# A retention-and-FFN kernel: scores of two rows in the FFN's PSUM banks, a new order in the attention bursts, and earlier loads of v

## The chip, the cores and the metric

The kernel runs on one core of a Trainium2 chip. The metric is the time of one execution on the device in microseconds (us); the figure of the kernel before is the median of three runs.

## The reference, cut to what matters

Inputs are q, k and v of shape (4 batches, 8 heads, 768 positions, 64) and two weight matrices, `w_in` (512 x 2048) and `w_out` (2048 x 512), all drawn in float32.

```python
for t in range(S):
    state = gamma * state + outer(k[t], v[t])       # per batch and head, 64 x 64
    y[t] = scale * q[t] @ state
x = y with the heads side by side                   # 3072 tokens x 512
h = x @ w_in
g = h * clip(h + 3.0, 0.0, 6.0) / 6.0
out = g @ w_out
```

## The kernel before, in words

**The work.** The 3072 tokens are cut into 24 rows of 128 (`NROW`), six rows to a batch (`ROWS_B`), and the rows into six units of four (`UR`, `NU`). The recurrence is done in chunks of 64 positions, two in a row: scores of k against q, a mask, products of masked scores with v (the inner part), products of q with the state from before (the outer part), and sums k x v that are added to the state. The FFN's first product is made for 16 blocks of 128 of the 2048 features and for six units of 512 tokens: 96 groups, each of 12 matmuls of 128x512 (`mm1`, L380: four blocks of the contraction times three products of a high and a low part). The second product (`mm2`, L479) is a blocked scheme with seven products per two units.

**The row's step.** `burst(r)` (L298) does the new part of row r and the old part of row r - 1 on TensorE. Its order before is: the outer part of the old row (`outer_part`, L232), a small matmul called `pace`, the scores of the new row (`scores`, L245), another `pace`, the inner part of the old row (`inner_part`, L257), then on VectorE `xr`, the old row's result times its decay (L321), split into a high part (ScalarE, L127) and a low part (VectorE, L128) of `x`; then the sums of the new row (`gather`, L269), the mask product `am` (VectorE, L335) and two additions to the state (`add_up`, L282: VectorE, L290; for the first row of a batch one copy on ScalarE, L292). Scores and sums of a row lie in one tile `sc` of two PSUM banks, from a pool with a single buffer.

**The FFN's first product.** `mm1` takes one tile `h` of one PSUM bank from the pool `ps_h`, which has three buffers (L90, L381). After its 12 matmuls ScalarE makes relu(h + 3) (L389), VectorE multiplies min(6 ., ...) by h (L390), and the result `g` is stored to DRAM. The next group's tile is another of the three buffers.

**Where the order comes from.** TensorE's order is written by hand: all of `advance` and `mm1` is issued in program order (L395). The first five bursts (rows 0 to 4) come before any group. The first four groups have a burst behind each of them. In units 0 and 1, whose 32 groups are interleaved, the bursts of rows 8 to 12 follow, in units 2 to 4 four bursts to a unit of 16 groups, and in unit 5 there are none. The other engines' orders are set when the program is built, by a scheduler that goes by the dependencies between tiles. All loads and stores are issued by SyncE.

**Early loads.** The first eight rows (`AHEAD`) are loaded at the start (`load`, L182): kt, qt, vn, kn of a row, 256 KB each, then the decay table `dq` of the row (`load_decay`, L213), and after rows 0, 2, 3 and 5 (`WITH`) one block of `w_in` of 512 KB (`fetch`, L96). For these rows ScalarE scales vn by a decay, eight instructions to a row (`decay`, L201). The blocks of `w_in` are turned into float32 and split (`build_w1`, L143: six instructions of VectorE and two of ScalarE); four of them are built between the first bursts, the others beside the groups.

Of the kernel before, what the change touches and what calls it, by code (L numbers as in the profile page):

```python
# [9 lines left out]
F32 = mybir.dt.float32  # L10
# [6 lines left out]
PSUM = bass.MemoryType.PSUM  # L17
DRAM = bass.MemoryType.DRAM

P = 128  # L20
# [8 lines left out]
def retention_ffn(ctx: ExitStack, tc: tile.TileContext, qkv, w_in, w_out, dvs, dqs, out, B, H, S, D):  # L29
# [6 lines left out]
    nc = tc.nc  # L36
# [6 lines left out]
    ROWS_B = S // P  # L43
    UR = 4
    UT = UR * P
    NU = NROW // UR
    WARM = 14
    AHEAD = 2 * UR
    WITH = (0, 2, 3, 5)
    BUFS = {"lkt": 1, "lqt": 2, "lvn": 2, "lkn": 1}  # L50
    SPARE = ("lkn", "lkt", "lqt", "lqt")
    BLK = 2 * P
# [11 lines left out]
    HALF = P // 2  # L64
# [11 lines left out]
    def nm(s):  # L76
        return f"{s}_{next(serial)}"
# [8 lines left out]
    ph1 = ctx.enter_context(ExitStack())  # L86
    wst = ph1.enter_context(tc.tile_pool(name="wst", bufs=1))
    xpool = ph1.enter_context(tc.tile_pool(name="xpool", bufs=2))
    hpool = ph1.enter_context(tc.tile_pool(name="hpool", bufs=3))
    ps_h = ph1.enter_context(tc.tile_pool(name="ps_h", bufs=3, space=PSUM))  # L90
    att = ctx.enter_context(ExitStack())
    apool = att.enter_context(tc.tile_pool(name="apool", bufs=2, side="right"))
    ps_a = att.enter_context(tc.tile_pool(name="ps_a", bufs=1, space=PSUM, side="right"))


    def fetch(src):  # L96
        st = wst.tile([P, src.shape[-1]], I64, tag="st", name=nm("st"), bufs=2)
        nc.sync.dma_start(out=st, in_=src)
        return st
# [69 lines left out]

    warm = apool.tile([P, 2, P], F32, tag="state", name="warm")  # L170
    nc.vector.memset(warm, 0.0)
    idle = ps_h.tile([P, UT], F32, tag="h", name="idle")
    for n in range(WARM):
        nc.tensor.matmul(idle[:, 0:P], warm[:, 0], warm[:, 1], start=True, stop=True)


    halves = [slice(h * D, (h + 1) * D) for h in range(2)]
# [4 lines left out]
    def load(r):  # L182

        t = rows[r] = {}
        if r < AHEAD and r % 2 == 0:
            early[r] = wpool.tile([P, 7, NPAIR, P], F32, tag="w", name=nm("early"), bufs=NSLOT - 1)
        for i, (x, n) in enumerate((("kt", 1), ("qt", 0), ("vn", 3), ("kn", 2))):  # L190
            o = r % 2 * 4 + i
            if r < AHEAD and o < 7:
                t[x] = early[r // 2 * 2][:, o]
            else:
                tag = SPARE[r // 2] if r < AHEAD else f"l{x}"
                t[x] = apool.tile([P, NPAIR, P], F32, tag=tag, name=nm(x), bufs=BUFS[tag])
            nc.sync.dma_start(out=t[x].rearrange("p h n -> p (h n)"), in_=qkv[r, n])
        if r >= AHEAD:
            decay(r)

    def decay(r):  # L201
        v = rows[r]["vn"].rearrange("p a (h e) -> p (a h) e", h=2)
        if r < AHEAD:
            for h in range(H):
                nc.scalar.activation(
                    out=v[:, h], in_=v[:, h], func=AF.Copy, scale=cst_sb[:, r % ROWS_B, h : h + 1]
                )
        else:
            nc.gpsimd.tensor_tensor(  # L209
                out=v, in0=v, in1=cst_sb[:, r % ROWS_B, :, None].to_broadcast([P, H, D]), op=ALU.mult  # L210
            )

    def load_decay(r):  # L213
        if r < AHEAD:
            if "dq" not in early:
                early["dq"] = wpool.tile([P, ROWS_B, NPAIR, P], F32, tag="w", name=nm("early"), bufs=NSLOT - 1)
            t = early["dq"][:, r % ROWS_B]
        else:
            t = apool.tile([P, NPAIR, P], F32, tag="dq", name=nm("dq"), bufs=1)
        rows[r]["dq"] = t  # L220
        if r < ROWS_B or r >= AHEAD:
            nc.sync.dma_start(out=t.rearrange("p h n -> p (h n)"), in_=dqs[r % ROWS_B])
# [22 lines left out]
    def scores(t):  # L245

        for i, c, a, h in tiles:
            nc.tensor.matmul(  # L248
                t["sc"][halves[h ^ a], a, i, c],
                t["kt"][halves[h], 2 * i + a, cut[c]],  # L250
                t["qt"][halves[h], 2 * i + a, cut[c]],
                start=True,
                stop=True,
                skip_group_check=True,
            )
# [13 lines left out]
    def gather(t, n):  # L269

        for i, c, a, h in tiles:
            if not c or n < ROWS_B - 1:
                nc.tensor.matmul(  # L273
                    t["u"][halves[h], a, c, i],
                    t["kn"][halves[h ^ a], 2 * i + a, cut[c]],
                    t["vn"][halves[h ^ a], 2 * i + a, cut[c]],
                    start=True,
                    stop=True,
                    skip_group_check=True,
                )  # L280
# [17 lines left out]
    def burst(r, new=True, old=True):  # L298

        new, old = new and rows.get(r), old and rows.get(r - 1)  # L300
        if old:
            ys = ps_a.tile([P, 2, UT], F32, tag="y", name=nm("y"))[:, :, 0 : 2 * P]
            old["y"] = ys.rearrange("p h (i n) -> p h i n", i=2)
            outer_part(old, (r - 1) % ROWS_B)
            pace()
        if new:
            sc = ps_a.tile([P, 2, 2, 4, HALF], F32, tag="sc", name=nm("sc"))
            new["sc"] = sc[:, :, 0].rearrange("p a (i c) n -> p a i c n", i=2)
            new["u"] = sc[:, :, 1].rearrange("p a (c i) n -> p a c i n", c=2)
            scores(new)  # L310
        if old:
            pace()
            inner_part(old)
            u, n = divmod(r - 1, UR)
            if u not in xs and u == 2:
                xs[u] = [wpool.tile([P, NK, UT], F32R, tag="w", name=nm("x"), bufs=NSLOT - 1) for a in range(2)]
            elif u not in xs:
                x = xpool.tile([P, 2, NK, UT], F32R, tag="x", name=nm("x"))
                xs[u] = [x[:, a] for a in range(2)]
            x = apool.tile([P, NPAIR, P], F32, tag="xr", name=nm("xr"))  # L320
            nc.vector.tensor_tensor(  # L321
                out=x.rearrange("p (h i) n -> p h (i n)", h=2),
                in0=ys,
                in1=old["dq"].rearrange("p (h i) n -> p h (i n)", h=2),
                op=ALU.mult,
            )
            hi, lo = (xs[u][a][:, :, n * P : (n + 1) * P] for a in range(2))
            split(hi, lo, x)
            del rows[r - 1]
        if new:  # L330
            gather(new, r % ROWS_B)
            if r in before:
                new["state"] = before.pop(r)
            new["am"] = apool.tile([P, 2, 2, 2, HALF], F32, tag="am", name=nm("am"), bufs=1)
            nc.vector.tensor_tensor(  # L335
                out=new["am"].rearrange("p a i c n -> p a (i c) n"),
                in0=sc[:, :, 0],
                in1=mask[:, None, None].to_broadcast([P, 2, 4, HALF]),
                op=ALU.mult,
            )  # L340
            add_up(r)

    def attention():

        st = []
        for r in range(AHEAD):
            load(r)
            load_decay(r)
            if r in WITH:
                st.append(fetch(w_in[len(st)]))  # L350
        decay(0)
        for r in range(NROW + 1):
            if r == AHEAD:
                burst(r, new=False)
                yield
                burst(r, old=False)
            else:
                burst(r)
            if st and r in (0, 2, 3, 4):
                build_w1(len(WITH) - len(st), st.pop(0))  # L360
            if r + 1 < AHEAD:
                decay(r + 1)
            if r >= AHEAD - 1 and r + 1 < NROW:
                load(r + 1)
            if AHEAD <= r < NROW:
                load_decay(r)
            yield

    gen = attention()
    done = 0  # L370

# [6 lines left out]


    def mm1(u, jj):  # L380
        h = ps_h.tile([P, UT], F32, tag="h", name=nm("h"))  # L381
        for k in range(NK):
            t, o = w1_block(jj, k)
            for n, (a, b) in enumerate(((0, 0), (0, 1), (1, 0))):
                nc.tensor.matmul(  # L385
                    h, t[:, o, a], xs[u][b][:, k], start=k + n == 0, stop=(k, n) == (NK - 1, 2), skip_group_check=True
                )
        g = hpool.tile([P, UT], F32, tag="g", name=nm("g"))
        nc.scalar.activation(out=g, in_=h, func=AF.Relu, bias=three)  # L389
        ins = nc.vector.scalar_tensor_tensor(out=g, in0=g, scalar=6.0, in1=h, op0=ALU.min, op1=ALU.mult)  # L390
        nc.sync.dma_start(out=gd[jj // 2][:, u, jj % 2], in_=g)
        return ins.ins
# [8 lines left out]
    advance(UR + 1)  # L401
    n_w1, n_w2 = len(WITH), 0
    for n, (u, jj) in enumerate(steps):
# [150 lines left out]
    for n, step in enumerate(work):  # L554
        b, s, j = step
# [95 lines left out]
```

## Time and profile before

| | |
|---|---|
| median of three runs (lowest, highest) | 593.75 us (593.53, 596.97) |
| the profiled execution | 594.2 us, of which the span of its instructions 592.4 us |
| TensorE matmul busy | 568.0 us, 96% of the span |
| VectorE busy | 438.1 us, 74% |
| ScalarE busy | 247.3 us, 42% |
| `mm1` matmuls (L385) | 1152, 271.1 us busy, from 32.2 to 355.2 us |
| `mm2` matmuls (L490) | 1008, 232.3 us busy, behind them |

The page's busy time of TensorE is modelled at its ends: a stream of matmuls overlaps, so 394 ns is the duration of one, not the step from one to the next. The idle time before an instruction is put down to what released it. Windows of the trace give the busy time of each engine in a stretch, with the clock that TensorE was granted (1.00 is full speed).

### The profile page before, as it was taken

The page shows a single profiled execution, that of the slowest core. Times are in us where ns is not written, and L with a number is a line of the kernel's source. Part 1 is how long each engine was busy: PE and PEld are TensorE (multiplying, and loading weights), DVE is VectorE, ACT ScalarE, POOL GpSimd, SP SyncE. Part 2 cuts the span into 40 slices and gives each one's busy share as a digit, 9 for nine tenths or more (in the row PEclk, how much of TensorE's full clock was granted, in tenths as well). Part 3 has the DMA queues.
Part 4 walks back from the last instruction along what each step waited for, and adds up shares of the span by engine and source line. Part 5 has one row for each costly group of instructions (what it writes and reads, how often), then busy time and mean ns, then how long its engine had stood idle before and what let it go on. Part 6 is the DMA issues. An engine that isn't in the chain of part 4 may idle for free.

```text
span 592.4 us, 13046 instructions
## 1 busy us (share of the span) xinstructions
PE 568.0 (96%) x5228; PEld 466.6 (79%) x5228; DVE 438.1 (74%) x790; ACT 247.3 (42%) x446; POOL 17.1 (3%) x22
## 2 busy tenths in 40 slices
PE   6787999898999999999999999999999999999997
PEld 5665788687888888888888886888888888888885
DVE  4869999999634499344436975999689966799853
ACT  5664445444322344222234544454444443444430
POOL 0001000000001000000000000000000000000000
PEclk8788999999999999999999999999999999999999
DMA  9966586665855557655445428984689635897002
GB/s 329 391 232 206 186 268 221 242 225 195 274 187 192 176 196 233 231 167 188 165 139 181 161 105 294 361 266 128 202 285 339 186 107 175 267 299 255 18 1 106
DMA packets 63564, 124.12 MB, mean 210 GB/s; under 512 B 7312, under 2 KB 7568, under 8 KB 63504
## 3 DMA queue, kind: packets, MB, share of 16 engines
q1 hardware_dynamic: 63216, 123.24, 61.9%
q8 instruction: 41, 0.67, 0.5%
q14 instruction: 19, 0.16, 0.1%
q10 hardware_dynamic: 288, 0.06, 0.0%
HBM read 91.81 MB, written 31.46 MB: 208 GB/s over the span
## 4 chain that ended last, share of the span: by engine, by line
PE 76%; DVE 16%; DMA 3%; issue 3%; ACT 1%; SPq 0%; DVEq 0%; ACTq 0%
PE o L490 38%; PE h L385 33%; DVE g L390 2%; DVE w L128 2%; DVE wb L115 2%; DVE we L118 2%; DVE ww L121 2%; PE y L236 1%; PE y L260 1%; PE sc L273 1%; PE sc L248 1%; DMA st<-in_w_in 1%; DVE we L109 1%; DVE wb L110 1%; DVE ws L80 1%
## 5 line engine op out<-in xcount | busy, mean ns | idle before, releaser
L385 PE MATMUL h<-x,w 128*128 128x512 f32 x1152 | 271.1, 394 | 4.7 <-DVE g L390 3.2
L385 PEld LDWEIGHTS h<-x,w 128*128 128x128 f32 x1152 | 215.2, 189 | 52.5 <-DVE g L390 4.7
L490 PE MATMUL o<-gc,w 128*128 128x512 f32 x1008 | 232.3, 392 | 1.4 <-ACT gc L127 1.0
L490 PEld LDWEIGHTS o<-gc,w 128*128 128x128 f32 x1008 | 189.1, 188 | 44.5 <-ACT gc L127 1.8
L390 DVE SCALAR_TENSOR_TENSOR g<-g,h 128x512 f32<-128x512 f32 x96 | 65.7, 685 | 80.7 <-ACT g L389 80.7
L389 ACT ACTIVATE g<-h,three 128x512 f32<-128x512 f32 x96 | 65.2, 684 | 97.4 <-PE h L385 91.6
L128 DVE TENSOR_TENSOR gc<-gr,gc 128x512 fp32r<-128x512 f32 x120 | 80.1, 691 | 22.1 <-ACT gc L127 21.8
L127 ACT ACTIVATE gc<-gr 128x512 fp32r<-128x512 f32 x120 | 71.9, 623 | 58.1 <-PE o L490 39.8
L127 ACT ACTIVATE gc<-keep 128x512 fp32r<-128x512 f32 x48 | 30.3, 633 | 62.8 <-PE o L490 45.0
L128 DVE TENSOR_TENSOR gc<-keep,gc 128x512 fp32r<-128x512 f32 x48 | 33.3, 695 | 13.5 <-ACT gc L127 13.4
L127 ACT ACTIVATE w<-ww 128x384 fp32r<-128x384 f32 (+2 forms) x34 | 18.8, 555 | 42.6 <-DVE ww L121 34.8
L113 ACT ACTIVATE we<-we,ebias 128x512 int32<-128x512 int32 x32 | 23.0, 718 | 20.2 <-DVE we L109 20.2
L127 ACT ACTIVATE x<-xr 128x512 fp32r<-128x512 f32 x24 | 15.1, 630 | 29.3 <-DVE xr L321 29.3
L507 DVE SCALAR_TENSOR_TENSOR u<-o,u 128x512 f32<-128x512 f32 (+1 forms) x31 | 20.1, 667 | 6.3 <-PE o L490 6.3
L209 POOL TENSOR_TENSOR vn<-vn,cst_sb 128x512 f32<-128x512 f32 x16 | 16.8, 1049 | 268.3 <-DMA vn<-in_qkv 268.3
L121 DVE SCALAR_TENSOR_TENSOR ww<-wb,we 128x512 f32<-128x512 f32 x32 | 22.8, 713 | 0.6
L115 DVE SCALAR_TENSOR_TENSOR wb<-st,wb 128x512 f32<-128x512 uint32 x32 | 22.9, 714 | 0.3
L335 DVE TENSOR_TENSOR am<-sc,mask 128x512 f32<-128x512 f32 x24 | 16.4, 684 | 8.5 <-PE sc L273 8.5
L128 DVE TENSOR_TENSOR w<-ww,w 128x384 fp32r<-128x384 f32 (+2 forms) x34 | 20.1, 594 | 3.3 <-ACT w L127 3.2
L118 DVE SCALAR_TENSOR_TENSOR we<-st,we 128x512 int32<-128x512 int32 x32 | 22.0, 687 | 0.1
L83 DVE TENSOR_TENSOR keep<-gr,gr 128x512 f32<-128x512 f32 x24 | 16.5, 694 | 5.7 <-DMA gr<-gd 5.7
L128 DVE TENSOR_TENSOR x<-xr,x 128x512 fp32r<-128x512 f32 x24 | 16.5, 688 | 2.7 <-ACT x L127 1.9
(48 smaller groups left out, 360.5 us busy)
## 6 DMA issues: line engine op xcount, KB each, us to landing
gr<-gd SPq DMA_DIRECT2D x168, 256.0 KB, 4.1
gd<-g SPq DMA_DIRECT2D x96, 256.0 KB, 2.7
st<-in_w_in SPq DMA_DIRECT2D x16, 512.0 KB, 4.3
st<-in_w_out SPq DMA_DIRECT2D x16, 512.0 KB, 4.4
early<-in_qkv SPq DMA_DIRECT2D x28, 256.0 KB, 6.0
kn<-in_qkv SPq DMA_DIRECT2D x20, 256.0 KB, 4.7
kt<-in_qkv SPq DMA_DIRECT2D x16, 256.0 KB, 4.3
qt<-in_qkv SPq DMA_DIRECT2D x16, 256.0 KB, 3.6
```

The lines of the kernel that those rows point to most:

```text
L113: nc.scalar.activation(out=e, in_=e, func=AF.Relu, scale=8.0, bias=ebias)
L115: nc.vector.scalar_tensor_tensor(out=y, in0=lo.bitcast(U32), scalar=2.0**-32, in1=b, op0=ALU.mult, op1=ALU.add)
L118: nc.vector.scalar_tensor_tensor(out=e, in0=hi, scalar=-2147483648, in1=e, op0=ALU.bitwise_and, op1=ALU.bitwise_or)
L121: nc.vector.scalar_tensor_tensor(out=w, in0=y, scalar=2.0**-20, in1=e.bitcast(F32), op0=ALU.mult, op1=ALU.mult)
L127: nc.scalar.activation(out=hi, in_=src, func=AF.Copy)
L128: nc.vector.tensor_tensor(out=lo, in0=src, in1=hi, op=ALU.subtract)
L209: nc.gpsimd.tensor_tensor(out=v, in0=v, in1=cst_sb[:, r % ROWS_B, :, None].to_broadcast([P, H, D]), op=ALU.mult)
L385: nc.tensor.matmul(h, t[:, o, a], xs[u][b][:, k], start=k + n == 0, stop=(k, n) == (NK - 1, 2), skip_group_check=True)
L389: nc.scalar.activation(out=g, in_=h, func=AF.Relu, bias=three)
L390: ins = nc.vector.scalar_tensor_tensor(out=g, in0=g, scalar=6.0, in1=h, op0=ALU.min, op1=ALU.mult)
L490: nc.tensor.matmul(banks[b, i, h], w2c[jj][:, RIGHT[i], a, h], gc[:, q, c], start=jj == 0 and n == 0, stop=jj == NFP - 1 and n == 2, skip_ ...
L507: nc.vector.scalar_tensor_tensor(out=out_[:, cut], in0=banks[b, i, h][:, cut], scalar=f, in1=other[:, cut], op0=ALU.mult, op1=ALU.add)
```

## The change

- Three one-bank tiles `h` become one tile `hs` of three banks, `[P, 3, 512]`, from the same pool with one buffer. `mm1` takes the slice `hs[:, n % 3]`, in turn. The warm-up matmuls write the third slice.
- Scores and sums of rows 1 and 3 lie in the first two slices of `hs`; all other rows keep the tile `sc`.
- A burst issues scores of the new row, outer part of the old row, `pace`, sums of the new row, `pace`, inner part of the old row.
- For rows 1 to 7 vn is loaded ahead of kt, qt and kn; `dq` of a row is loaded behind the next row's data; the blocks of `w_in` are fetched behind rows 1, 3, 4 and 6.

```diff
-    WITH = (0, 2, 3, 5)
+    WITH = (1, 3, 4, 6)
...
-    ps_h = ph1.enter_context(tc.tile_pool(name="ps_h", bufs=3, space=PSUM))
+    ps_h = ph1.enter_context(tc.tile_pool(name="ps_h", bufs=1, space=PSUM))
...
-    idle = ps_h.tile([P, UT], F32, tag="h", name="idle")
+    NH = 3
+    hs = ps_h.tile([P, NH, UT], F32, name="hs")
+    turns = iter(range(1 << 30))
     for n in range(WARM):
-        nc.tensor.matmul(idle[:, 0:P], warm[:, 0], warm[:, 1], start=True, stop=True)
+        nc.tensor.matmul(hs[:, NH - 1, 0:P], warm[:, 0], warm[:, 1], start=True, stop=True)
...
-        for i, (x, n) in enumerate((("kt", 1), ("qt", 0), ("vn", 3), ("kn", 2))):
-            o = r % 2 * 4 + i
+        parts = [("kt", 1), ("qt", 0), ("vn", 3), ("kn", 2)]
+        for i in (2, 0, 1, 3) if 0 < r < AHEAD else range(4):
+            (x, n), o = parts[i], r % 2 * 4 + i
...
         new, old = new and rows.get(r), old and rows.get(r - 1)
+        if new:
+            if r < UR and r % 2:
+                sc = hs[:, 0:2].rearrange("p a (b x n) -> p a b x n", b=2, n=HALF)
+            else:
+                sc = ps_a.tile([P, 2, 2, 4, HALF], F32, tag="sc", name=nm("sc"))
+            new["sc"] = sc[:, :, 0].rearrange("p a (i c) n -> p a i c n", i=2)
+            new["u"] = sc[:, :, 1].rearrange("p a (c i) n -> p a c i n", c=2)
+            scores(new)
         if old:
             ys = ps_a.tile([P, 2, UT], F32, tag="y", name=nm("y"))[:, :, 0 : 2 * P]
             old["y"] = ys.rearrange("p h (i n) -> p h i n", i=2)
             outer_part(old, (r - 1) % ROWS_B)
             pace()
         if new:
-            sc = ps_a.tile([P, 2, 2, 4, HALF], F32, tag="sc", name=nm("sc"))
-            new["sc"] = sc[:, :, 0].rearrange("p a (i c) n -> p a i c n", i=2)
-            new["u"] = sc[:, :, 1].rearrange("p a (c i) n -> p a c i n", c=2)
-            scores(new)
+            gather(new, r % ROWS_B)
         if old:
             pace()
             inner_part(old)
...
         if new:
-            gather(new, r % ROWS_B)
             if r in before:
                 new["state"] = before.pop(r)
...
             load(r)
-            load_decay(r)
+            if r:
+                load_decay(r - 1)
             if r in WITH:
                 st.append(fetch(w_in[len(st)]))
+        load_decay(AHEAD - 1)
         decay(0)
...
     def mm1(u, jj):
-        h = ps_h.tile([P, UT], F32, tag="h", name=nm("h"))
+        h = hs[:, next(turns) % NH]
```

How the change moves instructions is seen in the built programs' orders. In them a name is a tile with its number, `x16` counts equal rows that follow each other, and the brackets name the engines' counters for which a row waits (`DVE_49` is VectorE's, `Activation_49` ScalarE's, `PE_49` TensorE's own, `DMAHW` a transfer's).

The first place is TensorE from the end of the first group on, through the burst of row 5, to the second group. Before:

```order
L236 MATMUL y_638<-early_149,state_498 64x64 [waits PE_49]
L236 MATMUL y_638<-early_149,state_498 64x64 x3
L236 MATMUL y_638<-early_149,state_595 64x64 [waits DVE_49]
...
L230 MATMUL pace_655<-mask 64x4
L248 MATMUL sc_657<-early_149 64x64 [waits DMAHW6_49,DMAHW7_49,DVE_49,PE_49]
L248 MATMUL sc_657<-early_149 64x64 x15
L230 MATMUL pace_674<-mask 64x4 [waits PE_49]
L260 MATMUL y_638<-am_593,early_149 64x64 x16
L273 MATMUL sc_657<-early_149,kn_158 64x64 [waits DMAHW1_49,DMAHW0_49]
L273 MATMUL sc_657<-early_149,kn_158 64x64 x7
L385 MATMUL h_730<-x_286,w_20_229 128x512 x12
```

Now:

```order
L251 MATMUL sc_635<-early_146 64x64 [waits DMAHW6_49,DMAHW7_49,DVE_49,PE_49]
L251 MATMUL sc_635<-early_146 64x64 x15
L239 MATMUL y_652<-early_146,state_496 64x64 [waits PE_49]
...
L233 MATMUL pace_669<-mask 64x4
L276 MATMUL sc_635<-early_146,kn_157 64x64 [waits DMAHW5_49,DMAHW0_49]
L276 MATMUL sc_635<-early_146,kn_157 64x64 x7
L233 MATMUL pace_679<-mask 64x4 [waits PE_49]
L263 MATMUL y_652<-am_591,early_146 64x64 x16
L394 MATMUL hs<-x_301,w_20_229 128x512 [waits DVE_49]
L394 MATMUL hs<-x_301,w_20_229 128x512 x11
```

Scores moved to the front and sums ahead of the inner part; the second group, which waited for nothing of its own, now waits for VectorE. The count of VectorE's work that this wait names is reached with `g_631`, the `g` of the first group. So it is for every later group: in the built program the wait of each of the groups 2 to 96 names the count at which the `g` of the group just before it is finished. Before, a group's wait, where it has one, names the `g` of three groups earlier.

The second place is VectorE in the early rows, where `we`, `wb` and `ww` are the steps of building a block of `w_in`. Before, from the state of row 1 to that of row 2:

```order
L290 TENSOR_TENSOR state_309<-sc_251,state_218 128x256
L290 TENSOR_TENSOR state_311<-sc_251,state_309 128x256
L109 TENSOR_SCALAR we_402<-st_139 128x512
L110 TENSOR_SCALAR wb_401<-st_139 128x512
L115 SCALAR_TENSOR_TENSOR wb_401<-st_139,wb_401 128x512
L321 TENSOR_TENSOR xr_375<-y_321,early_123 128x512
L335 TENSOR_TENSOR am_395<-sc_340,mask 128x512
L290 TENSOR_TENSOR state_397<-sc_340,state_311 128x256
L128 TENSOR_TENSOR x_286<-xr_375,x_286 128x4x128
L290 TENSOR_TENSOR state_399<-sc_340,state_397 128x256
```

Now:

```order
L293 TENSOR_TENSOR state_308<-hs,state_218 128x256
L293 TENSOR_TENSOR state_310<-hs,state_308 128x256
L329 TENSOR_TENSOR xr_390<-y_337,early_128 128x512
L342 TENSOR_TENSOR am_394<-sc_320,mask 128x512
L293 TENSOR_TENSOR state_396<-sc_320,state_310 128x256
L128 TENSOR_TENSOR x_301<-xr_390,x_301 128x4x128
L293 TENSOR_TENSOR state_398<-sc_320,state_396 128x256
L109 TENSOR_SCALAR we_401<-st_144 128x512
L110 TENSOR_SCALAR wb_400<-st_144 128x512
L115 SCALAR_TENSOR_TENSOR wb_400<-st_144,wb_400 128x512
```

The second block's build moved behind the state of row 2. Up to the low part of `x` of row 3, which the first group needs, VectorE has the same instructions in both programs, three built blocks among them.

## The prediction

> **What bounds the kernel now.** I read the page first, then the busy time by stage, then the waits of TensorE, and last the timeline where one group of the first product follows another. From the page:
>
> ```profile
> PE 568.0 (96%) x5228; PEld 466.6 (79%) x5228; DVE 438.1 (74%) x790; ACT 247.3 (42%) x446; POOL 17.1 (3%) x22
> PEclk8788999999999999999999999999999999999999
> L385 PE MATMUL h<-x,w 128*128 128x512 f32 x1152 | 271.1, 394 | 4.7 <-DVE g L390 3.2
> ```
>
> TensorE is busy nearly all the time, and the 1152 matmuls of the first product lose only 4.7 us to waits, 3.2 of them to `g`. The stages (columns: stretch, its length, busy time of TensorE, of its weight loads, of VectorE, ScalarE, GpSimd, then TensorE's granted clock):
>
> ```profile
> 0.00:33.00 33.00, 22.08 (x605) 19.63 (x605) 20.13 (x39) 19.88 (x61) 0.34 (x6) 0.79 0.98 362
> 33.00:64.00 31.00, 26.16 (x492) 20.80 (x492) 28.09 (x51) 15.73 (x36) 2.16 (x2) 0.89 0.56 188
> 64.00:150.00 86.00, 82.53 (x887) 67.24 (x888) 85.25 (x174) 40.08 (x67) 3.14 (x3) 1.00 0.69 229
> 150.00:314.00 164.00, 163.93 (x2057) 136.01 (x2056) 86.58 (x157) 52.09 (x81) 11.48 (x11) 1.00 0.58 195
> 314.00:357.00 43.00, 43.00 (x191) 35.59 (x190) 33.02 (x71) 19.95 (x32) 0.00 (x0) 1.00 0.40 140
> ```
>
> The reader is to see three things. Before 33 us no engine is full: the early rows wait on each other. From 64 to 150 us TensorE and VectorE are both full. From 150 to 357 us TensorE never stops, and VectorE has room. So whatever puts an idle stretch between two groups of the first product lengthens the run by its whole size. How a group hands over to ScalarE and VectorE, in unit 5, where no burst lies between groups:
>
> ```profile
> 348.70 6.51 PE L385 MATMUL h<-x,w 128*128 128x512 f32 x28
> 349.80 0.69 ACT L389 ACTIVATE g<-h,three 128x512 f32<-128x512 f32 x1 [0.44 <-PE h L385]
> 352.52 0.69 ACT L389 ACTIVATE g<-h,three 128x512 f32<-128x512 f32 x1 [2.03 <-PE h L385]
> 355.24 0.69 ACT L389 ACTIVATE g<-h,three 128x512 f32<-128x512 f32 x1 [2.03 <-PE h L385]
> 355.97 0.69 DVE L390 SCALAR_TENSOR_TENSOR g<-g,h 128x512 f32<-128x512 f32 x1 [2.03 <-ACT g L389]
> ```
>
> ScalarE starts each 2.72 us after the last (349.80, 352.52, 355.24): that is a group of 12 matmuls, 0.227 us each. The last matmul ends at 348.70 + 6.51 = 355.21, ScalarE starts 0.03 later, VectorE 0.73 after ScalarE. All this runs beside the next group today, since that group writes another buffer.
>
> **The change part by part.** *One tile in place of three buffers.* The three banks are the same, and each group still takes the next bank. But the dependency is now that of one tile: the order shows the second group waiting for VectorE, where it waited for nothing, and the count named by each of the 95 waits is that of the `g` just before. A group may start only when ScalarE and VectorE have finished with the group ahead of it, though they read another bank. The work that hid this hand-over, the next group's matmuls, is the work that now waits. What a start behind such a wait looks like, VectorE's `g`, then TensorE, and one more start behind a wait:
>
> ```profile
> 135.88 0.68 DVE L390 SCALAR_TENSOR_TENSOR g<-g,h 128x512 f32<-128x512 f32 x1
> ```
>
> ```profile
> 136.61 5.74 PE L385 MATMUL h<-x,w 128*128 128x512 f32 x24 [1.63 <-DVE g L390]
> ```
>
> ```profile
> 361.68 0.50 PE L490 MATMUL o<-gc,w 128*128 128x512 f32 x1 [0.96 <-ACT gc L127]
> ```
>
> `g` ends at 136.56 and TensorE starts 0.05 later. The 24 matmuls take 5.74 us, where 23 steps of 0.227 and one duration of 0.39 make 5.60: a start behind a wait costs 0.14 (the third row, 0.50 in place of 0.39, says 0.11). I take 0.13. The step from one group to the next is then: 0.05 to start, 11 x 0.227 + 0.39 + 0.13 = 3.01 for the matmuls to the last one's end, 0.03, 0.73, and 0.68 of VectorE: 4.50 us, where it was 2.72. Each hand-over costs 1.78 us. Without the start cost it is 1.65, with one more VectorE instruction of 0.69 in front of `g` it is 2.47.
>
> *How many pay.* A burst between two groups covers the chain, if it is long enough:
>
> ```profile
> 160.38 11.18 PE L385 MATMUL h<-x,w 128*128 128x512 f32 x48
> 171.48 0.69 PE L236 MATMUL y<-qt,state 64*64 64x64 f32 x32
> 173.74 0.50 PE L385 MATMUL h<-x,w 128*128 128x512 f32 x1
> ```
>
> The burst lasts 173.74 - 171.48 = 2.26 us; from the last matmul's start the chain takes 0.39 + 0.03 + 0.73 + 0.68 + 0.05 = 1.88. It is covered, with 0.4 to spare. Of the 95 boundaries, 9 of the 31 in units 0 and 1 have a burst and 12 of the 48 up to the end of unit 4; the 16 into and in unit 5 have none. That leaves 22 + 36 + 16 = 74 without cover: 74 x 1.78 = 131.7 us. The 3.2 us that groups lose to `g` today are inside it and are taken off.
>
> *VectorE's own queue.* From 64 to 150 us VectorE is full today at 86 / 28 = 3.1 us a group. With 4.50 a group there is room, but the scheduler fills it with the building of weights, some 3.8 us between two `g`, which leaves nothing of the 3.82 between them. I add 0.2 for each of the 22 waits there, 4 us in all; bounds are 0 and a whole instruction of 0.69 for these and the 15 busy ones of unit 5, 25 us.
>
> *Scores first, sums ahead of the inner part.* TensorE issues the same matmuls and the same two `pace`. Behind row 8 all their inputs are long there: nothing gained or lost. Scores first have to wait until the row before has left `sc`; the inner part now has kn of the new row and its scaled vn ahead of it. Both fall in the first rows, which go with the loads:
>
> *Early rows and loads.*
>
> ```profile
> 7.66 0.69 DVE L335 TENSOR_TENSOR am<-sc,mask 128x512 f32<-128x512 f32 x1 [6.53 <-PE sc L273]
> ...
> 17.41 0.43 DVE L109 TENSOR_SCALAR we<-st 128x512 int32<-128x512 int32 x1 [1.99 <-DMA st<-in_w_in]
> ...
> 32.91 0.68 DVE L128 TENSOR_TENSOR x<-xr,x 128x512 fp32r<-128x512 f32 x1
> ```
>
> The first group needs `x` of row 3, finished at 33.59. Between 7.66 and 33 us VectorE is busy 20.13 - 0.27 = 19.9 of 25.3 us (the 0.27 is a memset), and up to that `x` it has the same instructions in both programs. So at most its 5.4 us of idle time can go. Of the waits, 2.0 are for the second block of weights, which comes four transfers later now but is built behind row 2's state, so that this one goes. New ones come: the first row's state copy stands behind 16 scalings on ScalarE, not 8, some 1.3 us for VectorE; the first block of weights is the eleventh transfer and not the seventh, about 1.1; and `xr` of row 1 stands behind outer part and sums, about 2. vn ahead of kt and qt brings the scalings forward by two transfers, and `dq`, four later, is still there before its row's `xr`. From 5.4 to about 4.7: I take 0.5 us gained, with bounds of 5 gained and 3 lost. The three estimates are from the loads' pace of the timeline (vn of row 2, the 15th, used at 14.7, the second weights, done with the 19th, at 17.4).
>
> *Sum* against the profiled execution: 592.4 + 131.7 - 3.2 + 4 - 0.5 = 724.4 us of span. The median stands 593.75 - 592.4 = 1.35 above that span, so the time is **726 us**, 22% slower. The second product is as before and comes later by the same amount.
>
> **The rivals.** *The clock falls as well.* TensorE would idle 1.49 us behind every uncovered group. Two pairs of neighbouring clock windows:
>
> ```profile
> 31.39:34.80 3.41, 1.91 (x10) 1.35 (x10) 2.50 (x6) 0.56 (x2) 0.00 (x0) 1.00 1.00 366
> 34.80:38.21 3.41, 3.41 (x28) 2.27 (x30) 2.11 (x4) 1.60 (x6) 0.00 (x0) 0.50 0.12 47
> 133.79:137.20 3.41, 1.78 (x9) 1.15 (x8) 3.38 (x9) 2.01 (x4) 0.94 (x1) 1.00 0.61 212
> 137.20:140.61 3.41, 3.41 (x17) 2.80 (x16) 3.34 (x8) 1.82 (x4) 0.00 (x0) 1.00 0.41 156
> ```
>
> TensorE busy 1.91 of 3.41 us, with small matmuls among them, was followed by a window at half clock; 1.78, all large, was not. A window that holds the whole new idle stretch has 1.92 busy: the rows leave it open. If each such window halves the next, with a chance of (3.41 - 1.49) / 3.41 = 0.56 at each of 74, and a half window loses some 1.4 us of work, it is 58 us more: 784; if only the 37 that VectorE's queue may delay do, 37 x 0.56 x 1.4 = 29 at most. For it: the early stages run at 0.79 and 0.89. Against: the three long waits for `g` of today, up to 1.63, left the clock at 1.00.
>
> The Trainium skill, page "TensorE: Matmul & The Clock Gate", section "A second HAM failure mode: psum-queue depth-cycling", says that short idle times between groups of matmuls that take PSUM banks in turn are enough to make the clock swing. Its section "Why this matters for your kernels" allows idle gaps up to about 3 us. By the first the time is this rival's, by the second it is the forecast; no run here shows either for a gap in every group.
>
> *VectorE hides the 22 waits of units 0 and 1.* Both engines are full there, so VectorE might set the pace anyway: 52 x 1.78 = 93 us, 687. Against it stands that TensorE is busy 82.5 of the 86 us too.
>
> *The three banks still turn as three buffers*, so that it is not slower. The place is the first matmul of each group. If the wait were for the `g` of three groups earlier, a chain of 4.50 would lie inside three groups of 2.72, each wait would be met long before, and only the early rows would be left: 593, or 589 at its bound. It decides from the count that the wait names, and that speaks against it. For it speaks that the data are in different banks.
>
> The Trainium skill, page "PSUM — Partial Sum Buffer", section "PSUM bank collisions raise a hardware error", has the rule that PSUM is to be guarded by bank and quadrant; by it these groups need no wait, and the sum is this rival's. The rule says what has to be guarded, and the order shows what is.
>
> **How the numbers follow.** The hand-over in every uncovered group, at full clock: 0.66, its own range 712 to 745 by the bounds of the start cost and of VectorE's queue. The clock falls, in part or in whole: 0.24. Hidden in units 0 and 1: 0.06. Three buffers after all: 0.04. The range from 708 to 772 takes in the clock's partial fall. A measurement of this kernel tells about 1% from no change: faster 0.01, within it 0.03, slower 0.96.
>
> **What would show it.** Right: in unit 5 ScalarE's starts 4.5 us apart instead of 2.72; TensorE's wait of L394 for `g` some 1.5 us, 74 times and about 110 us in all; bursts without a wait behind them; VectorE no longer full from 64 us on; the first product over near 487 us; the granted clock at 1.00. Wrong: starts 2.72 apart (three buffers), 0.50 in the clock's rows beyond 70 us (the clock), a pace of 3.1 us a group up to the end of unit 1 (hidden), or a first group that starts several us away from 33.6.

## The result, and the profile after

The changed kernel takes 741.28 us (median of four runs, 740.82 to 743.38) against 593.85 for the kernel before beside it: a ratio of 1.2475, interval 1.2427 to 1.2523. The forecast was 726, the range 708 to 772. The profiled execution took 740.82 us, of which the span is 739.0. From the page of the changed kernel:

```profile
PE 596.3 (81%) x5228; PEld 465.5 (63%) x5228; DVE 440.0 (60%) x790; ACT 248.5 (34%) x446; POOL 17.9 (2%) x22
PEclk8788999899999998999999999999999999999999
L394 PE MATMUL hs<-x,w 128*128 128x512 f32 x1152 | 299.7, 410 | 121.4 <-DVE g L399 119.3
```

The number of instructions is the same on every engine. TensorE is no longer full (81% where it was 96%), and no other engine has become so. The third row holds the answer: the matmuls of the first product stood idle for 121.4 us, 119.3 of them behind VectorE's `g`; before it was 4.7 and 3.2. The waits of TensorE (in all, times, longest) say how often:

```profile
PE hs L394 <- DVE g L399: 119.3, 76, 3.4
PE sc L251 <- DVE state L293: 4.0, 1, 4.0
PE y L239 <- DVE state L293: 3.9, 3, 1.9
```

The stages, cut as they now lie (columns as before: length, TensorE, its loads, VectorE, ScalarE, GpSimd, clock):

```profile
64.00:150.00 86.00, 60.32 (x531) 44.46 (x531) 80.11 (x163) 35.49 (x58) 2.81 (x2) 0.94 0.56 185
150.00:314.00 164.00, 122.19 (x1417) 92.15 (x1416) 61.14 (x114) 35.87 (x56) 7.32 (x8) 0.98 0.40 135
314.00:357.00 43.00, 32.48 (x362) 24.61 (x361) 11.31 (x19) 7.46 (x11) 3.11 (x3) 1.00 0.36 122
357.00:502.00 145.00, 104.00 (x832) 76.95 (x831) 55.01 (x106) 35.88 (x56) 2.09 (x2) 1.00 0.29 98
502.00:739.00 237.00, 231.99 (x1002) 188.72 (x1000) 185.53 (x304) 99.31 (x170) 0.00 (x0) 0.99 0.63 206
```

From 150 us to 502 TensorE is idle for a quarter of the time, VectorE for over three fifths and ScalarE for three quarters and more: no engine bounds these stages, the chain from one engine to the next does. The second product lasts nearly as long as it did. One turn of the chain, from the timeline of unit 5:

```profile
492.25 0.69 DVE L399 SCALAR_TENSOR_TENSOR g<-g,hs 128x512 f32<-128x512 f32 x1 [3.84 <-ACT g L398]
492.99 3.03 PE L394 MATMUL hs<-x,w 128*128 128x512 f32 x12 [1.50 <-DVE g L399]
496.06 0.69 ACT L398 ACTIVATE g<-hs,three 128x512 f32<-128x512 f32 x1 [3.84 <-PE hs L394]
496.78 0.69 DVE L399 SCALAR_TENSOR_TENSOR g<-g,hs 128x512 f32<-128x512 f32 x1 [3.85 <-ACT g L398]
500.59 0.69 ACT L398 ACTIVATE g<-hs,three 128x512 f32<-128x512 f32 x1 [3.85 <-PE hs L394]
501.31 0.69 DVE L399 SCALAR_TENSOR_TENSOR g<-g,hs 128x512 f32<-128x512 f32 x1 [3.85 <-ACT g L398]
```

Each engine's row names the one before it in the chain, and each waits until that one is done: VectorE ends at 492.94, TensorE starts at 492.99 and ends at 496.02, ScalarE starts at 496.06, VectorE at 496.78. From one `g` to the next it is 501.31 - 496.78 = 4.53 us, where it was 2.72. The last `g` starts at 501.31 us, where it started at 355.97: 145.3 us later.

### The profile page after: what moved, and what is told of

The parts are those of the page before. It is cut to its first block, busy times and chain, and to the rows that moved or that the text cites. A ratio compares the mean times of both kernels' runs of the same rounds, so it can differ in the third digit from the quotient of the medians.

```text
span 739.0 us, 13044 instructions
## 1 busy us (share of the span) xinstructions
PE 596.3 (81%) x5228; PEld 465.5 (63%) x5228; DVE 440.0 (60%) x790; ACT 248.5 (34%) x446; POOL 17.9 (2%) x22
## 4 chain that ended last, share of the span: by engine, by line
PE 51%; DVE 5%; ACT 4%; issue 1%; DMA 0%; DVEq 0%; SPq 0%
PE o L499 31%; PE hs L394 18%; DVE g L399 4%; ACT g L398 3%; PE y L263 1%; PE sc L251 1%; DMA gr<-gd 0%; PE y L239 0%; PE sc L276 0%; DVE w L128 0%; ACT w L127 0%; DVE ww L121 0%; DVE ws L80 0%; DVE gc L128 0%; DVE we L118 0%
## 5 line engine op out<-in xcount | busy, mean ns | idle before, releaser
L394 PE MATMUL hs<-x,w 128*128 128x512 f32 x1152 | 299.7, 410 | 121.4 <-DVE g L399 119.3
L394 PEld LDWEIGHTS hs<-x,w 128*128 128x128 f32 x1152 | 214.3, 193 | 198.8 <-DVE g L399 151.7
L399 DVE SCALAR_TENSOR_TENSOR g<-g,hs 128x512 f32<-128x512 f32 x96 | 66.0, 687 | 211.6 <-ACT g L398 211.3
L398 ACT ACTIVATE g<-hs,three 128x512 f32<-128x512 f32 x96 | 65.9, 687 | 235.3 <-PE hs L394 235.3
L113 ACT ACTIVATE we<-we,ebias 128x512 int32<-128x512 int32 x32 | 22.9, 715 | 14.7 <-DVE we L109 14.6
L208 ACT ACTIVATE early<-early,cst_sb 128x64 f32<-128x64 f32 x64 | 16.5, 334 | 3.3 <-DMA early<-in_qkv 3.3
```

Source lines behind the costliest of these rows:

```text
L113: nc.scalar.activation(out=e, in_=e, func=AF.Relu, scale=8.0, bias=ebias)
L394: nc.tensor.matmul(h, t[:, o, a], xs[u][b][:, k], start=k + n == 0, stop=(k, n) == (NK - 1, 2), skip_group_check=True)
```

## The experiments

The theory: three banks in one tile are one dependency, so that each group waits for the `g` of the group just before. The first rival is that something else in the change costs the time (two rows' scores in these banks, the order of the burst, the loads). The second is that the clock granted to TensorE carries a large part of it. The first four kernels ran on one chip, the other four together on another occasion; each ratio is against the runs of the kernel before that went with it (medians 594.86 and 595.17).

**The tile alone put back.** Everything else of the change stays, but `h` is again three tiles, and rows 1 and 3 use `sc`:

```diff
-    ps_h = ph1.enter_context(tc.tile_pool(name="ps_h", bufs=1, space=PSUM))
+    ps_h = ph1.enter_context(tc.tile_pool(name="ps_h", bufs=3, space=PSUM))
...
-        h = hs[:, next(turns) % NH]
+        h = ps_h.tile([P, UT], F32, tag="h", name=nm("h"))
```

> The changed kernel, but h is again three tiles of one bank, and rows 1 and 3 keep their scores in sc; new burst order and new loads stay. Theory (a group waits for the g just before it because all three slices are one tile): the 145 us vanish, steps of groups without a burst back at 2.72, time 590 to 597. Rival (the new order of the bursts or the later weights cost it): 650 or more.

597.48 us, ratio 1.0035 (1.0011 to 1.0058). The page's group of the first product:

```profile
L389 PE MATMUL h<-x,w 128*128 128x512 f32 x1152 | 269.3, 393 | 2.9 <-ACT x L127 1.4
```

The 119.3 us of waits for `g` are gone, and with them all of the loss but 2 to 3 us. So the tile carries it, alone or with the two rows' scores that went back with it; the kernel with a pool of its own, below, tells these apart.

**One line on the kernel before.** Its three buffers become one; order, loads and scores stay as they were:

```diff
-    ps_h = ph1.enter_context(tc.tile_pool(name="ps_h", bufs=3, space=PSUM))
+    ps_h = ph1.enter_context(tc.tile_pool(name="ps_h", bufs=1, space=PSUM))
```

> The kernel before with one line changed: the pool of h has one buffer, so all groups use the same bank. Theory: the same wait as in the change, steps of 4.53 without a burst and 5.20 with one, 738 to 746, although the banks no longer turn. Rival (it is the slices, the turning banks or the early rows of the change that cost): well under 700.

734.97 us, ratio 1.2353 (1.2288 to 1.2418). Its waits for `g`:

```profile
PE h L385 <- DVE g L390: 120.6, 77, 3.9
```

One bank used again and again costs what three banks in turn cost in the changed kernel: 77 waits and 120.6 us, against 76 and 119.3. That the groups of the change write different banks is worth nothing there. The time is 3 us below the range that was expected, and 6.3 below the changed kernel. The expected range was the changed kernel's own time. Of the 6.6 us between the two profiled spans, 2.2 are an earlier first `g` (36.61 us against 38.80), 3.3 lie between the first `g` and the last, and 1.1 in the second product.

**The whole change with a pool of its own for the two rows.** Rows 1 and 3 have two banks of their own, which are given back before the first group; `h` then has its three buffers:

```diff
-    ps_h = ph1.enter_context(tc.tile_pool(name="ps_h", bufs=1, space=PSUM))
+    few = ph1.enter_context(ExitStack())
+    ps_e = few.enter_context(tc.tile_pool(name="ps_e", bufs=1, space=PSUM))
...
-    hs = ps_h.tile([P, NH, UT], F32, name="hs")
+    hs = ps_e.tile([P, 2, UT], F32, name="hs")
...
+    few.close()
+    ps_h = ph1.enter_context(tc.tile_pool(name="ps_h", bufs=3, space=PSUM, reuse_waits="tile"))
```

> The whole change, but rows 1 and 3 use a two-bank tile of a pool of its own that is closed before the first group, and h is three tiles in the same banks. Theory: no wait between groups, 588 to 595; by the early rows' sum of the prediction about 593 (x of row 3 within 1 us of 33.7). Rival (something else in the change costs): above 600.

598.47 us, ratio 1.0059 (1.0035 to 1.0083). Scores in the groups' banks do not need the shared tile, and without it the change's other parts cost 3 to 4 us. They gain nothing.

**The gaps filled.** The changed kernel, with six matmuls into the `pace` bank behind each group of units 0 to 4 that has no burst behind it; nothing reads what they write:

```diff
+        was = done
...
+        if done == was and u < NU - 1 and (u, jj) != (NU - 2, NF - 1):
+            t, o = w1_block(jj, 0)
+            f = ps_a.tile([P, UT], F32, tag="pace", name=nm("fill"))
+            for k in range(6):
+                nc.tensor.matmul(f, t[:, o, 0], xs[u][0][:, 0], start=True, stop=True, skip_group_check=True)
```

> The change, with six more matmuls of 128x512 into the bank of pace behind each group of units 0 to 4 that has no burst behind it (their result is not used). They take 1.4 us of TensorE inside an idle stretch of 1.5. Theory of the clock (the 10 us above the sum are windows at half clock that idle stretches bring): no half-clock window beyond 75 us, steps 4.53 still, time 727 to 733. Rival (the 10 us are VectorE's queue): 740 or more.

737.87 us, ratio 1.2403 (1.2357 to 1.2449): 3.4 us less than the change, not the 8 to 14 that the clock's part had been put at. The intervals of the two ratios overlap a little, so that the 3.4 is an uncertain size. The same stages as above, of this kernel:

```profile
64.00:150.00 86.00, 78.51 (x629) 60.20 (x628) 80.25 (x164) 36.14 (x59) 2.72 (x2) 1.00 0.59 195
150.00:314.00 164.00, 156.95 (x1574) 121.25 (x1573) 60.92 (x114) 35.86 (x57) 8.66 (x8) 0.99 0.41 133
```

TensorE is busy 78.51 of 86 us and runs at 1.00 where it ran at 0.94, and still most steps from one `g` to the next without a burst are 4.51 to 4.57 us. So the step of 4.5 us does not come from TensorE's idling or its clock, it is the chain; the clock is a small second part, taken apart below.

**Two buffers.** The kernel before with two:

```diff
-    ps_h = ph1.enter_context(tc.tile_pool(name="ps_h", bufs=3, space=PSUM))
+    ps_h = ph1.enter_context(tc.tile_pool(name="ps_h", bufs=2, space=PSUM))
```

> The kernel before with two one-bank buffers of h in place of three. Theory (a group waits for the g of the group that last held its tile): the hand-over of 4.53 us from group start to the end of g now has to fit into two groups, 2 x 2.72 = 5.44 us, so it is hidden and the time stays at 594 to 600 us, ScalarE's starts in unit 5 stay 2.72 us apart, and the sum of waits for g stays below 10 us. Rival (each buffer less costs its share of the 145 us): about 665 us, with waits for g near 60 us.

600.55 us, ratio 1.0100 (1.0066 to 1.0134). Its waits for `g`, and the last three starts in unit 5:

```profile
PE h L385 <- DVE g L390: 6.0, 6, 1.7
```

```profile
351.68 0.69 ACT L389 ACTIVATE g<-h,three 128x512 f32<-128x512 f32 x1 [2.03 <-PE h L385]
354.40 0.69 ACT L389 ACTIVATE g<-h,three 128x512 f32<-128x512 f32 x1 [0.44 <-PE h L385]
357.12 0.69 ACT L389 ACTIVATE g<-h,three 128x512 f32<-128x512 f32 x1 [2.03 <-PE h L385]
```

The starts are 2.72 us apart again. A chain of 4.53 fits into two groups of 2.72, as the theory has it. The time is half a us above the range expected. The third buffer buys the 1% that is left: 2.8 us of it are longer waits for `g` (6.0 against 3.2), the rest was not traced. The loss is no share per buffer: from three to two it is about 5 us, from two to one about 135.

**The other parts one by one.** The tiles put back and the early banks had shown that order, loads and banks together cost a little. Three more kernels split that. The order alone, on the kernel before:

```diff
+        if new:
+            sc = ps_a.tile([P, 2, 2, 4, HALF], F32, tag="sc", name=nm("sc"))
...
+            scores(new)
         if old:
...
         if new:
-            sc = ps_a.tile([P, 2, 2, 4, HALF], F32, tag="sc", name=nm("sc"))
...
-            scores(new)
+            gather(new, r % ROWS_B)
...
         if new:
-            gather(new, r % ROWS_B)
```

> The kernel before with only the new order in a burst (scores, outer part, sums, inner part); three buffers, one sc, loads as before. Theory (scores first must wait until the row before has left the single sc): 596 to 599 us, the first g 3 to 6 us later than 38.5. Rival (the loads are what costs): within 1 us of the kernel before, first g at 38 to 39.

The loads alone, on the kernel before:

```diff
-    WITH = (0, 2, 3, 5)
+    WITH = (1, 3, 4, 6)
...
+        for i in (2, 0, 1, 3) if 0 < r < AHEAD else range(4):
...
-            load_decay(r)
+            if r:
+                load_decay(r - 1)
...
+        load_decay(AHEAD - 1)
```

> The kernel before with only the new loads (v ahead of k and q, decay tables and blocks of weights one row later); three buffers and the old order in a burst. Theory (the order is what costs): within 1.5 us of the kernel before, first g at 37 to 39.5. Rival (the loads cost, since blocks of weights come four transfers later): 596 to 599 us, first g 2 us or more later.

And the kernel of the early banks with the old loads, that is order and banks:

```diff
-    WITH = (1, 3, 4, 6)
+    WITH = (0, 2, 3, 5)
...
-        for i in (2, 0, 1, 3) if 0 < r < AHEAD else range(4):
+        for i, (x, n) in enumerate((("kt", 1), ("qt", 0), ("vn", 3), ("kn", 2))):
...
-            if r:
-                load_decay(r - 1)
+            load_decay(r)
...
-        load_decay(AHEAD - 1)
```

> The new order in a burst, rows 1 and 3 in two banks of their own that are given back before the first group, h with three buffers, loads as before. Theory (the order costs by the wait for sc, which the second pair of banks takes away): 593 to 596 us, first g within 1.5 us of 38.5, and 1 to 4 us ahead of the order alone. Rival (the banks gain nothing, since the rows go with the loads): the same time as the order alone within 1 us.

Measured: the order alone 598.42 us, ratio 1.0056 (1.0028 to 1.0084); the loads alone 596.27, ratio 1.0022 (0.9996 to 1.0048), no difference that can be told; order and banks 599.47, ratio 1.0082 (1.0057 to 1.0108). The order costs about 3 us. The banks were to undo that, and this expectation fell: they give nothing back. What may keep them from it is seen in the busy time up to 64 us and from there to 150. Kernel before:

```profile
0.00:64.00 64.00, 48.24 (x1097) 40.44 (x1097) 48.22 (x89) 35.61 (x97) 2.50 (x8) 0.84 0.78 278
64.00:150.00 86.00, 82.53 (x887) 67.24 (x888) 85.25 (x174) 40.08 (x67) 3.14 (x3) 1.00 0.69 229
```

The order alone:

```profile
0.00:64.00 64.00, 43.74 (x1016) 37.85 (x1016) 45.93 (x87) 34.92 (x95) 2.71 (x8) 0.76 0.77 277
```

Order and banks:

```profile
0.00:64.00 64.00, 44.59 (x1085) 38.59 (x1086) 44.25 (x84) 34.22 (x94) 3.21 (x8) 0.79 0.78 274
```

From 64 us VectorE is full (85.25 of 86), so what it has not done by then it still owes. It had done 48.22 us of work in the kernel before, 45.93 with the new order, 44.25 with order and banks: behind by 2.3 and 4.0. The last `g` of the two:

```profile
358.75 0.69 DVE L391 SCALAR_TENSOR_TENSOR g<-g,h 128x512 f32<-128x512 f32 x1 [2.03 <-ACT g L390]
```

```profile
361.08 0.69 DVE L395 SCALAR_TENSOR_TENSOR g<-g,h 128x512 f32<-128x512 f32 x1 [2.03 <-ACT g L394]
```

With 355.97 before, they start 2.8 and 5.1 us later. The first `g` (38.51, 45.25, 41.45; with both it came later than expected) says nothing of it: the banks bring it 3.8 us forward against the order alone, and the end comes later. The loads alone:

```profile
0.00:64.00 64.00, 46.88 (x1096) 40.49 (x1097) 48.47 (x90) 35.34 (x97) 2.95 (x8) 0.87 0.80 279
```

VectorE had done 48.47 here, and the last `g` came 1.6 us later. With the early banks of above it had done 44.59, and the last `g` came 3.4 later; with the tiles put back 47.92, and it came 2.4 later. So the rule holds to some 2 us. TensorE is nearly full from 64 us as well (82.53 of 86), and had done less by then in each of the three kernels shown (43.74, 44.59 and 46.88 against 48.24); no run tells the two engines apart. These are single profiled executions, and executions of one kernel differ by some 4 us either way; that the order holds VectorE up in the early rows is what they suggest, and only the ratios above are shown.

## Why the prediction was right, and where it was short

**The dependency.** Right: every group waits for the `g` just before. Putting back the tiles took the time away, one buffer in the kernel before brought it.

**How many pay.** 74 were forecast, as 22 in units 0 and 1, 36 in units 2 to 4 and 16 in unit 5. The trace has 24, 36 and 16. The two more are waits of 0.37 and 0.41 us behind bursts; the 74 without a burst all waited, 1.50 us or more. Bursts cover the chain as worked out: steps with a burst stayed at 5.20 and 4.97.

**The price of one.** Forecast 4.50 for a step, measured 4.53: 1.81 for a hand-over instead of 1.78. The 0.03 lies in the start of TensorE behind a wait (3.03 + 0.05 in place of 3.01 + 0.05) and in single hundredths. Over 74 this is 2 us.

**VectorE's queue.** 4 us were added for 22 waits, 0.2 each, from a pace of 86 / 28 = 3.1 us a group; 26 groups and not 28 have their `g` in that stretch, which makes it 3.3. For these 22 the size was right and the shape was wrong: they are 4.3 us over the plain 1.50. Where the sum had put nothing, units 2 to 4 are 2.8 over it and unit 5 is 0.4, so that the 74 together are 7.5 over. Of the 76 waits 65 are between 1.4 and 1.6 us, and the six over 1.7 (2.43, 2.40, 3.17, 1.84, 2.30, 3.44) hold 6.6 us over the plain 1.5 between them. The cause is visible in VectorE's timeline of the changed kernel ahead of the longest:

```profile
288.38 0.68 DVE L329 TENSOR_TENSOR xr<-y,dq 128x512 f32<-128x512 f32 x1
288.98 0.68 DVE L342 TENSOR_TENSOR am<-sc,mask 128x512 f32<-128x512 f32 x1
289.58 0.42 DVE L293 TENSOR_TENSOR state<-sc,state 128x256 f32<-128x256 f32 x1
...
291.49 0.69 DVE L128 TENSOR_TENSOR w<-ws,w 128x512 fp32r<-128x512 f32 x1
292.10 0.68 DVE L399 SCALAR_TENSOR_TENSOR g<-g,hs 128x512 f32<-128x512 f32 x1
```

What stands in front of `g` is not one instruction, it is a burst's whole follow-up and pieces of a weight block, without a gap. The prediction spread the delay over the waits of units 0 and 1; it sits at a few groups, three of the six right behind a step with a burst, and two of them at the start of unit 3.

**The clock: the term that was missing.** The sum had no loss of clock in it, and this is what was left out of it: half windows, stretches of some 3.4 us in which TensorE was granted half its clock. The waits in question, and the matmuls behind them:

```profile
67.79 4.58 PE L394 MATMUL hs<-x,w 128*128 128x512 f32 x12 [2.43 <-DVE g L399]
...
127.90 5.49 PE L394 MATMUL hs<-x,w 128*128 128x512 f32 x12 [3.17 <-DVE g L399]
...
275.62 4.25 PE L394 MATMUL hs<-x,w 128*128 128x512 f32 x12 [2.30 <-DVE g L399]
...
292.84 4.42 PE L394 MATMUL hs<-x,w 128*128 128x512 f32 x12 [3.44 <-DVE g L399]
```

Twelve matmuls take 3.03 us; these took 4.58, 5.49, 4.25 and 4.42, together 6.6 us more. The clock in those stretches:

```profile
68.88:72.29 3.41, 3.41 (x9) 2.20 (x7) 3.05 (x6) 1.24 (x2) 0.00 (x0) 0.50 0.61 201
126.90:130.30 3.40, 2.40 (x6) 1.92 (x7) 3.38 (x7) 1.24 (x2) 1.23 (x1) 0.50 0.64 246
130.30:133.70 3.40, 3.09 (x8) 1.89 (x6) 2.17 (x4) 0.27 (x1) 0.04 (x1) 0.50 0.32 98
277.10:280.50 3.40, 2.78 (x7) 1.66 (x5) 2.92 (x7) 1.83 (x3) 0.00 (x0) 0.50 0.05 8
294.20:297.60 3.40, 3.06 (x8) 1.87 (x6) 3.09 (x9) 0.30 (x1) 0.00 (x0) 0.50 0.56 169
```

So the rival of the falling clock was right in kind and wrong in where it falls: it had each hand-over of 1.5 us as a chance for a half window (58 us), and not one of the 65 plain ones was followed by one. Four of the five waits of 2.3 us and more were. The kernel with the gaps filled fits: at the second place the wait behind the fillers is 1.80 and the step 5.18 in place of 6.98; its one half window beyond 70 us follows its longest wait. The four steps with these waits take 3.5 us less there (6.07, 6.98, 5.75 and 5.92 became 4.87, 5.18, 5.08 and 6.10; the last is the one whose window stayed), and its own late start takes some of that back (its first `g` came 1.3 us later).

One more half window of the change lies at the start of the second product, from 509.20 us on, behind waits of 1.12 and 0.23 us for `gc`. From the last `g` to the end the four kernels with such a window there take 237.7 to 238.3 us, the other six 236.0 to 236.8. So this window carries most of the 1.3 us by which the second product is longer.

**Early rows.** Forecast a gain of 0.5 with 3 lost as the bound. The `x` of row 3 was done at 33.72 instead of 33.59, and the ratios of the parts put the loss at 2 to 4 us where the handing-over is not in the way. What the prediction left out is the stretch behind the first group: it looked at VectorE's idle time before 33 us for the first group's sake, and the single profiles above suggest that the work done by 64 us counts more.

**The sum.** From the first `g` to the last it is 145.05 us longer (501.31 - 38.80 against 355.97 - 38.51): 74 x 1.81 = 133.9, 6.6 for the clock and 7.5 for the queue make 148.0; the 3.2 us of earlier waits come off, which leaves 144.8, 0.2 short. That rest is a balance of things not priced one by one: the first four steps alone are 1.6 longer. The forecast for the same stretch was 131.7 + 4 - 3.2 = 132.5. The second product's part is 237.7 us against 236.4, and the first `g` came 0.3 later where 0.5 earlier was forecast: 12.6, 1.3 and 0.8 are the 14.6 us by which the span of 739.0 exceeds the forecast 724.4. Without the two losses of clock the time would be some 733 us, so that the range holds by the hand-over alone. Of the signs that were named, two came only in part: VectorE was still busy for 80.11 of the 86 us from 64 us on, and rows of 0.50 did come beyond 70 us.

The Trainium skill, page "TensorE: Matmul & The Clock Gate", section "Why this matters for your kernels", allows idle gaps between bursts of matmuls of up to about 3 us. This trace agrees that gaps of 1.5 us leave the clock alone, and differs on the bound: 2.30 and 2.43 were enough for a half window. The section "A second HAM failure mode: psum-queue depth-cycling" of the same page of the Trainium skill lets the clock swing from short idle times between groups alone; no plain hand-over here shows it.

## What to carry to other kernels

Count buffers by what the dependency goes by, here the tile, not by banks: one tile over several banks, written in turn, acted as one buffer. The price of a lost buffer is the chain (matmuls, then each reader in turn) less the time of a group, and it falls on every group that has no other work on TensorE behind it; as soon as the chain fits into the groups that the buffers span, more of them buy little. Where an engine is full from some point on, look also at how much work the engine has done when it gets there, not only at when the first group starts; the profiles here suggest this, to some 2 us, and do not show it.

## What the runs showed of the hardware that was not expected

In the first product, from 64 us on, the clock fell only behind waits for `g` well over the plain hand-over, in four kernels alike. In the changed kernel 65 waits for `g` of 1.4 to 1.6 us had no half window behind them, four of five of 2.3 and more had one. With one buffer, 63 waits of that plain size had none, and its four half windows beyond 70 us follow waits of 2.01, 2.34, 2.30 and 3.87 us, while one of 3.13 left the clock at full speed. With the gaps filled, the one window follows a wait of 2.12, and with the new loads alone one of 1.99. No wait for `g` up to 1.94 us had one.

What decides among the long waits can be read from the traces. The half windows begin at 68.88, 126.91, 277.10 and 294.16 us, which is 17, 44 and 5 times 3.413 us apart. Cut on that grid, the window ahead of the first of them and the one in which the wait of 2.40 us begins are:

```profile
65.47:68.88 3.41, 1.09 (x5) 0.92 (x6) 3.41 (x8) 1.82 (x3) 0.00 (x0) 1.00 0.50 186
89.36:92.77 3.41, 1.79 (x8) 1.13 (x6) 3.34 (x5) 1.32 (x3) 1.47 (x1) 1.00 0.38 101
```

The first holds nearly the whole wait of 2.43, TensorE is busy for 1.09 us in it, and the next window is at half clock. The wait of 2.40, from 91.15 to 93.55, lies across two windows, and the clock stayed. So did the 3.13 of the one buffer. In all ten traces some 960 such windows at full clock lie between 64 us and the end of the first product: the ten with TensorE busy for 1.48 us or less were each followed by one at half clock, and none of the others, from 1.66 us up, was. The window of 1.92 that the prediction left open is among those: 46 windows of the changed kernel with less than 1.95 left the next at full speed. So in this stretch it is the idle time inside one window that counts, not the length of the wait. The bound is not a general one: the early row of 1.91 in the prediction, with small matmuls, was followed by a half window, and so was the window from 505.79 to 509.20 us at the start of the second product, with 2.06 busy.
